# Moving the plain values of three batches behind the next scores, with other PSUM tiles for them and for the output, and a new order of VectorE's copies at the start

## The chip, the cores and the metric

The kernel runs on one core of one Trainium2 chip. A core has TensorE (PE: matrix products, with PEld its weight loads), VectorE (DVE), ScalarE (ACT), GpSimd (POOL) and SyncE (SP); each works through its own instructions in order, and semaphores hold one back until another has come far enough. Products are written to PSUM, eight banks of 2 KB in each of 128 partitions. The metric is device time in microseconds of one launch; the median of 3 runs of the kernel before is 308.29 us (308.21 to 308.9).

## The reference

Eight batches, 8 heads, 576 positions, head size 64: attention, then a two-layer network on all 4608 rows.

```python
rel = pos[:, None] - pos[None, :]
mask_plain = (rel >= 0) & (rel < 32)
mask_dil = (rel >= 0) & (rel < 32 * 4) & (rel % 4 == 0)
masks = np.stack([mask_plain if h < H // 2 else mask_dil for h in range(H)], axis=0)
scores = np.where(masks, scale * q @ k.T, -1e9)
attn = softmax(scores) @ v                  # each head
x = attn.transpose(0, 2, 1, 3).reshape(B * S, H * D)
h = x @ w_in                                # 512 -> 2048
out = (h * sigmoid(h)) @ w_out              # 2048 -> 512
```

Heads 0 to 3 see the last 32 positions ("plain"), heads 4 to 7 every fourth of the last 128 ("class": positions of one residue by four, where the mask is again a band of 32).

## The kernel before, in words

Each batch `b` has two halves of attention, `z` = 0 (plain) and `z` = 1 (class). A half goes through these steps:

- `scores(b, z)` (L500): 72 or 80 small products on TensorE with 64 rows and 32 columns of weights, into three tiles of the pool `ps`; VectorE then scales, masks and takes the maxima (L521 to L537).
- `exps` (L552) on ScalarE; `normal` (L574) on VectorE: reciprocal of the sums, then `pn`.
- `pn` is transposed to `pt`: for early batches on TensorE (`turn` L589, with the copy `turned` L598), later by a DMA on SP's queue (`turn_by_dma` L604).
- `values(b, z)` (L613): 64 small products, 64 by 64, of `pt` and `vw` into two tiles `x`, and by `last_values` (L679) 8 (plain) or 16 (class) more for the last 64 positions into two short tiles `xs`. `finish` (L709) and `last_finish` (L702) copy the four tiles into `xT`, the input of the network.

The network: `layer1(b, f)` (L721), `f` from 0 to 15, makes 8 products of 288 columns into a tile `h`, and ScalarE writes SiLU of it to `gT` (L734). `layer2(b, plan)` (L783) makes output tiles of 128 rows, `t`, counted by `x`: 16 products of 512 columns each into `o`; `store` (L777) copies `o` with VectorE (L780), and SP writes it out. Rows go by pairs of batches, so an even batch has four output tiles and an odd batch five.

The order is written by hand. `plan_of(b)` (L820) lists what else is issued in batch `b`: `at(s, fn, ...)` puts a call at step `s`; step `f` comes before `layer1(b, f)` (L1025), and steps from 16 on come before every fourth product of layer 2, four steps to an output tile (L795). At one step the calls run in the order of their `at`. TensorE runs layer 1 and 2 of batch `b` and, between their products, the attention of batches `b` + 1 and `b` + 2. In batches 3 to 5 that is: plain values of `b` + 1 at step 6 (L913), class scores of `b` + 1 at step 11 or 12, plain scores of `b` + 2 at step 17 (L920), class values of `b` + 1 at step 29 (L927), `normal` and `turn_by_dma` of the class half at steps 22 and 23 and of the plain half of `b` + 2 at 27 and 28 (L932).

PSUM is shared by two pools: `big` has two tiles of two banks (`h`, `o`, of which `o` uses the first bank), `ps` four tiles of one bank (scores, values). A tile that takes over a bank waits until the last reader of the tile there has finished.

Batch 0 starts with the attention of 288 rows in two parts (`masks0`, `scores0`, `values0` L642, `finish0` L670), while the weights are still on their way. `short_products` (L432) are small products of zeros that keep TensorE busy; 102 open the kernel (L942), and 14 stand before the sixth pair of `h` tiles (L1008). `shift_plain` (L195) is two copies on VectorE (L198, L200) that lay `v` beside itself for overlapping windows; in batch 0 the second set is at step -14 (L835), ahead of the copy `turned` at step -4 (L837).

Of the kernel before, what the change touches and what calls it, by code (L numbers as in the profile page):

```python
# [9 lines left out]
F32 = mybir.dt.float32  # L10
# [5 lines left out]
P = 128  # L16
# [4 lines left out]
QB = 32  # L21
# [8 lines left out]
def kernel(  # L30
# [10 lines left out]
    B, H, S, D = q.shape  # L41
# [7 lines left out]
    NM = NB // 2  # L49
# [4 lines left out]
    SA = NS // 2  # L54
# [555 lines left out]
            out=pt[:, 0 : w // 2], in_=a["pn", z, hi][:, 0:w].rearrange("p t c -> p (t c)")  # L610
        )

    def values(b, z):  # L613

        a = att(b)
        x = a["x", z] = [
            ps.tile([P, 2, SA], F32, tag="ps", name=f"x_{b}_{z}_{e}") for e in (0, 1)
        ]
        for i in range(8):
            for n in (0, 1):  # L620
                for e in (0, 1):
                    r = slice(e * KB, e * KB + KB)
                    for hi in (0, 1):
                        dst = x[e][hi * D : hi * D + D, n]
                        pt = a["pt", z, hi]
                        if z == 0:
                            j = 2 * i + e
                            w = plain_v(a, j, 2 * n + hi)
                            dst = dst[:, i * QB : (i + 1) * QB]
                            p = pt[r, 2 * n + j // 8, i % 4 * QB : i % 4 * QB + QB]  # L630
                        else:
                            m, c = i // 4, i % 4
                            w = class_v(a, 2 * m + e, 2 * n + hi, c)
                            dst = dst[:, m * P : (m + 1) * P].rearrange("d (i r) -> d r i", r=DIL)[:, c]
                            p = pt[r, 2 * n + m, c * QB : c * QB + QB]
                        nc.tensor.matmul(dst, w, p, start=True, stop=True)  # L636
        a["xs", z] = [
            ps.tile([P, 2, QB], F32, tag="ps", name=f"xs_{b}_{z}_{e}") for e in (0, 1)
        ]
        last_values(b, z, (0, 1))  # L640

    def values0(z, part):  # L642
# [134 lines left out]
    def store(o, row, name, m0=0, copy=nc.vector.tensor_copy, queue=nc.sync):  # L777
# [2 lines left out]
        copy(ob, o)  # L780
        queue.dma_start(out=out[row : row + P, m0 : m0 + m], in_=ob)

    def layer2(b, plan):  # L783

        tiles = range(0, 4) if b % 2 == 0 else range(4, 9)
        for x, t in enumerate(tiles):
            row = (b // 2) * 2 * S + t * P
            cut = 3 * DM // 4 if (b, t) == (B - 1, 8) else DM
            for m0, m1 in ((0, cut), (cut, DM)):
                if m0 == m1:  # L790
                    continue
                o = big.tile([P, 2, 512], F32, tag="big", name=f"o_{b}_{t}_{m0}")[:, 0, 0 : m1 - m0]
                for f in range(NFF):
                    if f % 4 == 0 and m0 == 0:
                        plan(NFF + 4 * x + f // 4)  # L795
                    nc.tensor.matmul(  # L796
                        o, gT[:, f, t * P : (t + 1) * P], w_out16[:, f, m0:m1],
                        start=(f == 0), stop=(f == NFF - 1),
                    )
                store(o, row, f"ob_{b}_{t}_{m0}", m0)  # L800
# [19 lines left out]
    def plan_of(b):  # L820
        ev = {}

        def at(s, fn, *args):
            ev.setdefault(s, []).append((fn, args))

        def all_exps(b, z):
            for hi in (0, 1):
                at(16, exps, b, z, hi)

        if b == 0:  # L830

            at(-14, normal, 0, 1, 1)
            at(-14, normal, 0, 0, 1)
            at(-14, shift_class, 0, dve, 1, 2)
            at(-14, shift_plain, 0, dve, 4, NM)  # L835
            at(-4, turn, 0, 0, 1)
            at(-4, turned, 0, 0, 1)  # L837
            at(-4, values0, 1, 1)
            at(-4, last_values, 0, 1, (1,))
            at(-4, finish0, 1, 1)  # L840
            at(-4, last_finish, 0, 1, 1)
            at(-2, values0, 0, 1)
            at(-2, last_values, 0, 0, (1,))
            at(-2, finish0, 0, 1, both)
            at(-2, last_finish, 0, 0, 1)
            at(-2, clear_short, 1, nc.vector)
            at(-2, load_v, 1)
            for c in (2, 3):
                at(-2, load_w_out, c)
            at(-2, load_qk, 2)  # L850
            transposes(at, 1, 1, 2)
            at(8, scores, 1, 1)
            for hi in (0, 1):
                at(8, shift, 1, 1, hi)
            for which in (1, 0):
                at(18, transpose, 1, 0, which, (dve, dve) if which else (act, act))
            at(20, normal, 1, 1, 0)
            at(20, scores, 1, 0)
            at(14, shift_v, 1, nc.sync.dma_start)
            at(18, load_rows, 3)  # L860
            at(18, load_v, 2)
            all_exps(1, 1)
            for hi in (0, 1):
                at(20, exps, 1, 0, hi)
            for n, z, hi in ((20, 1, 1), (26, 0, 0), (28, 0, 1)):
                at(n, normal, 1, z, hi)
            for n, z, copies in ((27, 1, (dve, dve)), (30, 0, both)):
                for hi in (0, 1):
                    at(n, turn, 1, z, hi)
                for hi in (0, 1):  # L870
                    at(n, turned, 1, z, hi, copies[hi])
                at(n + 1 + z, values, 1, z)
                at(n + 1 + z, finish, 1, z, both)
        elif b == 1:
            transposes(at, 2, 0, 3)
            transposes(at, 2, 1, 11)
            at(2, shift_v, 2, nc.sync.dma_start)
            for z in (0, 1):
                at(2, cross, 3, z)
                at(28, cross, 4, z)  # L880
            at(9, scores, 2, 0)
            for hi in (0, 1):
                at(12, shift, 2, 0, hi)
            at(17, load_v, 3)
            at(17, nc.gpsimd.tensor_copy, latch, qTs[1][:, 1, S - 1 : S])
            at(17, load_rows, 4)
            at(14, scores, 2, 1)
            all_exps(2, 0)
            all_exps(2, 1)
            for hi in (0, 1):  # L890
                at(19, normal, 2, 0, hi)
            at(21, scores, 3, 0)
            at(21, exps, 3, 0, 0)
            at(21, exps, 3, 0, 1)
            later(at, 2, 0, (None, None, 27, 28))
            later(at, 2, 1, (29, 31, 33, 34))
        else:
            if b + 2 < B:
                at(0, load_v, b + 2)
                if b + 3 < B:  # L900
                    at(0, load_rows, b + 3, (1, 0))
                if b + 3 < B:
                    at(12, cross, b + 3, 0)
                if b > 2:
                    at(12, cross, b + 2, 1)
            if b + 1 < B:
                at(1 if b == 2 else 0, shift_plain, b + 1, dve, 0, NM)
                at(12, shift_class, b + 1, dve, 0, 2)
                at(12, shift_over, b + 1, dve)
                if b == 2:  # L910
                    later(at, 3, 0, (0, 0, 4, 6))
                else:
                    at(6, values, b + 1, 0)  # L913
                    at(6, finish, b + 1, 0)
                x = {2: 13, 3: 12}.get(b, 11)
                at(x, scores, b + 1, 1)
                at(x, shift, b + 1, 1, 1)
                all_exps(b + 1, 1)
            if b + 2 < B:
                at(18 if b == 2 else 17, scores, b + 2, 0)  # L920
                for hi in (0, 1):
                    at(18, exps, b + 2, 0, hi)
            if b + 1 < B:
                for hi in (0, 1):
                    at(22 + hi, normal, b + 1, 1, hi)
                    at(22 + hi, turn_by_dma, b + 1, 1, hi)
                at(29, values, b + 1, 1)  # L927
                at(29, finish, b + 1, 1)
            if b + 2 < B:
                for hi in (0, 1):  # L930
                    at(27 + hi, normal, b + 2, 0, hi)
                    at(27 + hi, turn_by_dma, b + 2, 0, hi)  # L932

        def plan(s):
            for fn, args in ev.pop(s, ()):
                fn(*args)

        return plan


    busy = big.tile([P, 2, 512], F32, tag="big", name="busy")
    short_products(busy, 102)  # L942
    keep_busy(busy[:, 0], 8)
    masks0(1, 0)
    masks0(0, 0)
# [55 lines left out]
    for b in range(B):  # L1001
        plan = plan_of(b)
        if b == 0:
            for x in range(NFF):
                h = first[x] if x < 4 else None
                if x == 5:
                    h = big.tile([P, 2, 512], F32, tag="big", name=f"h_0_{2 * x}_0")
                    short_products(h, 14)  # L1008
                plan(2 * x - NFF)
                plan(2 * x + 1 - NFF)  # L1010
                tile = 2 * x % NFF, 2 * x // NFF
# [51 lines left out]
```

## Time and profile before

| What | Value |
|---|---|
| Median of 3 runs | 308.29 us |
| The profiled execution | 308.48 us, its span 306.7 us |
| PE busy | 298.1 us |
| ACT busy | 186.7 us |
| DVE busy | 180.8 us |
| Granted TensorE clock | 1.000 |
| Layer 1, products of L726 | 896, 113.5 us |
| Layer 2, products of L796 | 528, 114.3 us |
| Output copies of L780, VectorE | 35, mean 673 ns |

The span runs from the first to the last instruction of one execution that the hardware profiler recorded. Times of rows are microseconds from its start. A row of the timeline has start, length, engine, line, operation, out<-in, shape of the weights, shape of the output or operands, count, and in brackets how long the engine had been idle and what ended that. TensorE overlaps products, so lengths of its rows overlap, and a difference of two starts is what a run of products takes. An arrow like "<-PE o L796" names the instruction that released the wait.

### The profile page before, as it was taken

What the parts mean: (1) busy time and instruction counts of PE and PEld (TensorE: products, weight loads), DVE (VectorE), ACT (ScalarE), POOL (GpSimd) and SP (SyncE); (2) the same over time, 40 slices, a digit from 0 to 9 for tenths busy, and PEclk for the clock granted to TensorE, in tenths of its full rate; (3) what the DMA queues carried; (4) which work ended last, traced back from release to release, by engine and by line L of the source; (5) the groups of instructions that cost most, each with busy time, mean ns of one, the idle gap of its engine ahead of it and who ended that gap; (6) DMA issues with size and microseconds to landing.
All of it is one profiled execution on the core that took longest, in us unless ns stands there. A gap on an engine that the chain in (4) does not pass through costs nothing.

```text
span 306.7 us, 10605 instructions
## 1 busy us (share of the span) xinstructions
PE 298.1 (97%) x4591; PEld 189.2 (62%) x4591; DVE 180.8 (59%) x375; ACT 186.7 (61%) x554; POOL 92.3 (30%) x139
## 2 busy tenths in 40 slices
PE   8788999999999999999999999999999999999995
PEld 4466754677555875477644775467644775478543
DVE  7898579618797738953785348852885344620012
ACT  1757677776894558945792558945793558246200
POOL 8517455861462840096007610040000000000000
PEclk9999999999999999999999999999999999999999
DMA  8999999999999998499789995498026000400021
GB/s 105 169 204 203 189 205 203 154 211 179 148 151 192 163 202 108 128 149 175 104 152 169 194 118 105 130 139 118 4 75 145 34 4 7 139 36 2 3 100 71
DMA packets 104399, 39.00 MB, mean 127 GB/s; under 512 B 79504, under 2 KB 99600, under 8 KB 104352
## 3 DMA queue, kind: packets, MB, share of 16 engines
q0 software_dynamic: 63104, 18.88, 62.1%
q1 hardware_dynamic: 41248, 19.44, 29.3%
q8 instruction: 36, 0.59, 0.8%
q14 instruction: 11, 0.09, 0.1%
HBM read 37.75 MB, written 9.44 MB: 154 GB/s over the span
## 4 chain that ended last, share of the span: by engine, by line
PE 82%; DVE 9%; ACT 3%; DMA 3%; issue 1%; POOL 1%; POOLq 0%; SPq 0%; ACTq 0%
PE h L726 36%; PE o L796 29%; PE o L770 5%; PE h L746 4%; PE x L636 3%; DMA nat<-in_k_dram 2%; ACT pe L569 2%; DVE pn L585 2%; PE s L391 1%; DVE l L578 1%; PE s L379 1%; PE t L329 1%; DMA ptT<-pn 1%; DVE ms L521 1%; PE pt L594 1%
## 5 line engine op out<-in xcount | busy, mean ns | idle before, releaser
L734 ACT ACTIVATE gT<-h 128x576 f16<-128x576 f32 x112 | 72.9, 651 | 78.1 <-PE h L726 77.9
L796 PE MATMUL o<-w_out,gT 128*128 128x512 f16 (+2 forms) x528 | 114.3, 373 | 0.1
L726 PE MATMUL h<-xT,w_in 128*128 128x288 f16 x896 | 113.5, 286 | 0.0
L726 PEld LDWEIGHTS <-w_in 128*128 128x128 f16 x896 | 86.4, 98 | 23.3 <-DVE xT L713 0.3
L796 PEld LDWEIGHTS <-gT 128*128 128x128 f16 x528 | 50.0, 98 | 55.8 <-issue 0.3
L569 ACT ACTIVATE pe<-ms,nm 128x64 f32<-128x64 f32 x178 | 59.1, 333 | 2.8 <-DVE nm L537 2.7
L780 DVE COPY ob<-o 128x512 f32<-128x512 f32 (+2 forms) x35 | 23.5, 673 | 47.1 <-PE o L796 46.1
L521 DVE SCALAR_TENSOR_TENSOR ms<-s,mask 128x512 f32<-128x512 f32 x28 | 19.2, 685 | 35.5 <-PE s L391 24.7
L569 ACT ACTIVATION_READ_ACCUMULATOR pe<-ms,nm 128x1 f32 x178 | 33.2, 187 | 0.0
L713 DVE CAST xT<-x 128x512 f16<-128x512 f32 x26 | 16.8, 684 | 21.3 <-PE xs L700 21.3
L177 POOL DMA_DIRECT2D vw<-in_v_dram x16 | 10.1, 638 | 62.9 <-PE xs L700 62.0
L585 DVE TENSOR_TENSOR pn<-pe,r 128x640 f16<-128x640 f32 (+2 forms) x32 | 25.3, 791 | 1.1
L537 DVE TENSOR_REDUCE nm<-ms 128x10 f32<-128x640 f32 (+1 forms) x28 | 22.0, 787 | 1.0
L746 PE MATMUL h<-xT,w_in 128*128 128x256 f16 (+1 forms) x128 | 17.1, 286 | 0.8 <-DMA w_in<-in_moe_w_in_dram 0.6
L134 POOL DMA_DIRECT2D nat<-in_q_dram x20 | 14.8, 761 | 6.4 <-DMA nat<-in_k_dram 3.3
L134 POOL DMA_DIRECT2D nat<-in_k_dram x20 | 15.1, 760 | 5.0 <-DMA vw<-in_v_dram 3.8
L770 PE MATMUL o<-w_out,gT 128*128 128x512 f16 x64 | 15.2, 380 | 0.0
L746 PEld LDWEIGHTS <-w_in 128*128 128x128 f16 x128 | 11.8, 98 | 4.3 <-DMA w_in<-in_moe_w_in_dram 1.2
L758 ACT ACTIVATE gT<-h 128x512 f16<-128x512 f32 (+1 forms) x16 | 10.0, 653 | 6.0 <-PE h L746 5.8
L636 PEld LDWEIGHTS <-vw 64*64 64x64 f16 x896 | 8.5, 108 | 5.4 <-issue 5.3
L185 POOL DMA_DIRECT2D vw<-in_v_dram x16 | 9.3, 584 | 4.1 <-DVE r L582 1.7
L578 DVE TENSOR_REDUCE l<-pe 128x10 f32<-128x640 f32 (+2 forms) x12 | 9.6, 801 | 1.5 <-ACT pe L560 1.4
(102 smaller groups left out, 254.1 us busy)
## 6 DMA issues: line engine op xcount, KB each, us to landing
out_dram<-ob SPq DMA_DIRECT2D x35, 256.0 KB, 2.5
vw<-in_v_dram POOLq DMA_DIRECT2D x8, 288.0 KB, 7.8
vw<-in_v_dram POOLq DMA_DIRECT2D x16, 128.0 KB, 6.0
w_in<-in_moe_w_in_dram POOLq DMA_DIRECT2D x4, 512.0 KB, 12.9
w_out<-in_moe_w_out_dram POOLq DMA_DIRECT2D x4, 512.0 KB, 10.9
nat<-in_k_dram POOLq DMA_DIRECT2D x6, 256.0 KB, 7.5
nat<-in_q_dram POOLq DMA_DIRECT2D x6, 256.0 KB, 7.9
nat<-in_k_dram POOLq DMA_DIRECT2D x20, 72.0 KB, 7.2
```

The lines of the kernel that those rows point to most:

```text
L134: nc.gpsimd.dma_start(out=f[:, 2 * (1 - which) + h // 2, 0 : ZR - 1, h % 2], in_=src[b, h].rearrange("(m p) d -> p m d", p=RT),)
L521: nc.vector.scalar_tensor_tensor(out=ms[:, 0:8].rearrange("p (n t) c -> p n (t c)", n=2), in0=s[hi].rearrange("p n t c -> p n (t c)"), sca ...
L537: nc.vector.tensor_reduce(out=nm[:, 0:w], in_=ms[:, 0:w], axis=AX.X, op=ALU.max, negate=True)
L569: nc.scalar.activation(pe[:, t, :], slot(t), AF.Exp, scale=1.0 if b else scale, bias=nm[:, t : t + 1], accum_out=l[:, t : t + 1],)
L585: nc.vector.tensor_tensor(pn[:, 0:w], a["pe", z, hi][:, 0:w], r[:, 0:w, None].broadcast_to([P, w, KB]), ALU.mult)
L636: nc.tensor.matmul(dst, w, p, start=True, stop=True)
L726: nc.tensor.matmul(h[:, half, 0:HS], w_in16[:, c, f * P : f * P + P], xT[:, c, half * HS : half * HS + HS], start=(c == 0), stop=(c == MC ...
L734: nc.scalar.activation(gT[:, f, s0 : s0 + S].rearrange("p (a c) -> p a c", a=2), h[:, :, 0:HS], AF.Silu)
L746: nc.tensor.matmul(h[:, i, 0 : c1 - c0], w_in16[:, c, (f + i) * P : (f + i + 1) * P], xT[:, c, c0:c1], start=(c == 0), stop=(c == MC - 1),)
L770: nc.tensor.matmul(o, gT[:, f, t * P : (t + 1) * P], w_out16[:, f, :], start=(f == 0), stop=(f == NFF - 1),)
L780: copy(ob, o)
L796: nc.tensor.matmul(o, gT[:, f, t * P : (t + 1) * P], w_out16[:, f, m0:m1], start=(f == 0), stop=(f == NFF - 1),)
```

## The change

1. In batches 3, 4 and 5 (`merged`), `values(b + 1, 0)` goes from step 6 to step 17, right behind `scores(b + 2, 0)`, and its `finish` to step 24. Its two tiles `x` become the two banks of one `big` tile, and its first short tile `xs` lies in the second bank of the `big` tile that holds the first output tile.
2. In these batches output tiles 1 and 2 are taken from `ps`, and the fifth (`x` = 4, in batches 3 and 5) is the second bank of the tile whose first bank is the fourth output tile. So the output of such a batch takes two `big` tiles in place of four or five, and the values take one more.
3. There, `normal` and `turn_by_dma` of the second plain half of `b` + 2 go from step 28 to 30.
4. In batch 0 the second `shift_plain` goes from step -14 to -4, behind `turned`; `finish0(1, 1)` uses ScalarE for one of its two copies.
5. 100 short products open the kernel in place of 102, and the 14 before the sixth pair of `h` tiles are dropped.

```diff
+    pair = [None]
-    def values(b, z):
+    def values(b, z, beside=False):
         a = att(b)
-        x = a["x", z] = [
-            ps.tile([P, 2, SA], F32, tag="ps", name=f"x_{b}_{z}_{e}") for e in (0, 1)
-        ]
+        if beside:
+            both_x = big.tile([P, 2, 512], F32, tag="big", name=f"x_{b}_{z}")
+            x = [both_x[:, e].rearrange("p (n c) -> p n c", n=2) for e in (0, 1)]
+        else:
+            x = [ps.tile([P, 2, SA], F32, tag="ps", name=f"x_{b}_{z}_{e}") for e in (0, 1)]
+        a["x", z] = x
...
-        a["xs", z] = [
-            ps.tile([P, 2, QB], F32, tag="ps", name=f"xs_{b}_{z}_{e}") for e in (0, 1)
-        ]
+        if beside:
+            xs = [pair[0][:, 1, 0 : 2 * QB].rearrange("p (a c) -> p a c", a=2)]
+        else:
+            xs = [ps.tile([P, 2, QB], F32, tag="ps", name=f"xs_{b}_{z}_0")]
+        a["xs", z] = xs + [ps.tile([P, 2, QB], F32, tag="ps", name=f"xs_{b}_{z}_1")]
...
+    def merged(b):
+        return 2 < b < B - 2
...
-                o = big.tile([P, 2, 512], F32, tag="big", name=f"o_{b}_{t}_{m0}")[:, 0, 0 : m1 - m0]
+                if merged(b) and x in (1, 2):
+                    o = ps.tile([P, 512], F32, tag="ps", name=f"o_{b}_{t}")
+                elif merged(b) and x == 4:
+                    o = pair[0][:, 1]
+                else:
+                    pair[0] = big.tile([P, 2, 512], F32, tag="big", name=f"o_{b}_{t}_{m0}")
+                    o = pair[0][:, 0, 0 : m1 - m0]
...
-            at(-14, shift_plain, 0, dve, 4, NM)
             at(-4, turn, 0, 0, 1)
             at(-4, turned, 0, 0, 1)
+            at(-4, shift_plain, 0, dve, 4, NM)
...
-            at(-4, finish0, 1, 1)
+            at(-4, finish0, 1, 1, both)
...
-                else:
+                elif not merged(b):
                     at(6, values, b + 1, 0)
                     at(6, finish, b + 1, 0)
...
                 at(18 if b == 2 else 17, scores, b + 2, 0)
+                if merged(b):
+                    at(17, values, b + 1, 0, True)
+                    at(24, finish, b + 1, 0)
...
-                    at(27 + hi, normal, b + 2, 0, hi)
-                    at(27 + hi, turn_by_dma, b + 2, 0, hi)
+                    step = 27 + (3 if merged(b) else 1) * hi
+                    at(step, normal, b + 2, 0, hi)
+                    at(step, turn_by_dma, b + 2, 0, hi)
...
-    short_products(busy, 102)
+    short_products(busy, 100)
...
-                if x == 5:
-                    h = big.tile([P, 2, 512], F32, tag="big", name=f"h_0_{2 * x}_0")
-                    short_products(h, 14)
```

## The prediction

> **What bounds the kernel now.** I read the page first: the busy shares, the slices and the chain.
>
> ```profile
> span 306.7 us, 10605 instructions
> ...
> PE 298.1 (97%) x4591; PEld 189.2 (62%) x4591; DVE 180.8 (59%) x375; ACT 186.7 (61%) x554; POOL 92.3 (30%) x139
> ...
> PEclk9999999999999999999999999999999999999999
> ...
> PE 82%; DVE 9%; ACT 3%; DMA 3%; issue 1%; POOL 1%; POOLq 0%; SPq 0%; ACTq 0%
> ```
>
> TensorE is busy 97% of the span at full clock, and the slices below 9 lie in the first 20 us. So from about 30 us on, a change is worth what it takes from or adds to TensorE's own row of products and gaps; before that, which wait ends last. Next I read TensorE's timeline over batch 4, the middle one of the three that change.
>
> ```profile
> 174.83 0.69 PE L636 MATMUL x<-ptT,vw 64*64 64x32 f16 x64
> 175.36 0.22 PE L700 MATMUL xs<-ptT,vw 64*64 64x32 f16 x8
> 175.51 5.08 PE L726 MATMUL h<-xT,w_in 128*128 128x288 f16 x40
> ...
> 186.24 1.03 PE L796 MATMUL o<-w_out,gT 128*128 128x512 f16 x4
> 187.19 0.72 PE L379 MATMUL s<-plain 64*32 64x64 f16 x64
> 187.74 0.27 PE L379 MATMUL ss<-plain 64*32 64x64 f16 x8
> 187.94 10.53 PE L796 MATMUL o<-w_out,gT 128*128 128x512 f16 x48
> 198.40 0.71 PE L636 MATMUL x<-ptT,vw 64*64 64x32 f16 x64
> 198.93 0.32 PE L700 MATMUL xs<-ptT,vw 64*64 64x16 f16 x16
> 199.19 2.76 PE L796 MATMUL o<-w_out,gT 128*128 128x512 f16 x12
> 201.79 4.45 PE L726 MATMUL h<-xT,w_in 128*128 128x288 f16 x35
> ```
>
> The reader is to subtract starts, since a row's own length holds the drain. A product of layer 2 takes 0.216 us (199.19 to 201.79 for 12) and one of layer 1 0.1225 (15.68 us for the 128 that start at 270.40). The 4 products at 186.24 need 0.95 before the scores start, where 4 x 0.216 is 0.86: 0.09 us goes on entering the small tiles, at every such block. Leaving them costs 0.11 to 0.12 from the last small product's start.
>
> **Part 1: plain values behind the scores (batches 3, 4, 5 as b).** 72 small products leave step 6 of layer 1 and stand behind the 72 of the scores. Their own 0.68 us (174.83 to 175.51) is only moved. The entry at step 6 goes, 0.09. The step from the 64x32 tiles of the scores to the 64x64 tiles of the values takes the place of the scores' exit. No row shows that pair. The nearest is 64x128 to 64x64 at 6.6 us, where the last transpose is followed after 0.12 us; the other end is the 0.01 us between small products of one shape. I take 0.12, as the nearest in kind: nothing gained there, and 3 x 0.09 = **0.28 us gained** (at the other end 3 x 0.20 = 0.6). [...]
>
> What waits on them? With 0 at the first product of layer 2 (186.24), scores start at 0.96 and values at 1.65, end at 2.33, and output tiles then end at 4.92, 8.37, 11.82 and, with 0.79 of strided values inside, 16.15. On VectorE the four copies into xT (1.54 us by the rows from 199.65) now stand behind the second tile's copy: the first tile's copy starts at 5.1, the two class normalisations end at 9.15 (195.18 before, 0.2 later by the first tile's copy), second copy 9.75, xT copies 11.3, first plain normalisation 12.4, third copy 13.1. The strided values' second short tile takes the third tile's bank and is reached at 13.3: 0.2 us to spare. The strided xT copies end at 15.05, and the second plain normalisation, now at step 30, at 16.3, just as the fourth tile is ready (16.35). So VectorE is full but not late: cost nothing, 0.2 to 0.5 us a batch if the cover goes. Nothing else is queued behind it that TensorE wants earlier. That normalisation's transpose keeps its place on SP between the same two output stores. It lands 3.4 to 7.3 us after issue (four such rows), so by 24; its reader comes at 26.5 in batch 6 and much later in the others. The moved values and copies issue no DMA, and POOL's v loads wait for the strided values as before.
>
> **Part 2: output tiles in other banks.** Tiles 1 and 2 sit in one-bank tiles that the score copies have freed by 2.5 and 3.8; they start at 4.9 and 8.4. The fifth tile, in batches 3 and 5 only, goes into the second half of the large tile that holds the fourth. I read the order of the changed program with its waits: the fifth tile's first product waits for VectorE, for the copy of the fourth tile out of the other half. In before it waited for the copy of the tile two places earlier, long done. So TensorE now sits out a whole copy:
>
> ```profile
> 201.99 0.69 DVE L780 COPY ob<-o 128x512 f32<-128x512 f32 x1 [0.80 <-PE o L796]
> ```
>
> This copy, out of a last tile, starts 0.20 us after TensorE's next product did (201.79). 0.20 + 0.69 + 0.05 to wake TensorE (a copy that ends at 27.52 lets products start at 27.58, below) = 0.94 us idle. All of TensorE's queue is behind it, and the later batches follow TensorE, so nothing takes it up. Twice: **1.88 us lost**. It can't be much below 0.94 unless the wait is not there; above it by what VectorE is late (to 1.2).
>
> **Part 3: the start.** The timeline from 24 to 31 us tells it; VectorE's rows, then TensorE's:
>
> ```profile
> 25.81 0.42 DVE L205 COPY vw<-vw 32x1024 f16<-32x1024 f16 x1
> 26.15 0.48 DVE L198 COPY vw<-vw 32x1280 f16<-32x1280 f16 x1
> 26.64 0.48 DVE L200 COPY vw<-vw 32x1280 f16<-32x1280 f16 x1
> 27.05 0.47 DVE L602 COPY ptT<-pt 128x640 f16<-128x640 f16 x1
> ```
>
> ```profile
> 27.58 0.30 PE L700 MATMUL xs<-ptT,vw 64*64 64x16 f16 x8 [0.72 <-DVE ptT L602]
> 27.81 1.05 PE L746 MATMUL h<-xT,w_in 128*128 128x256 f16 x8
> ```
>
> The short values at 27.58 want a bank that the copy of pt gives back, and that copy stands behind two shifts of v, 0.90 us. In the change the copy goes first: pt is written at 26.27, the copy runs 26.31 to 26.78, and the values start at 26.83 instead of 27.58: 0.75. The shifts then end at 27.7 and one xT copy moves to ScalarE, which idles from 27.24 to 28.89, so VectorE ends this row at 28.3 instead of 28.45. With the rows' own distances (0.23 to the 8 products at 27.81, 0.98 to the next values, 0.43 and 0.88 to the first products of the second part) the next values start at 28.04 and the second part at 29.35 (30.10 before); VectorE's xT is ready at 29.2 (29.95 before). w_in's last quarter landed at 26.61 and the q for the transposes that move to 30.5 at 29.52. What TensorE waits for up to 60 us otherwise hangs on ScalarE or VectorE behind TensorE, and moves along; the nearest DMA margins there are over 1 us. So **0.75 us gained**, between 0 (a wait I have not seen takes it) and 0.8. The 14 short products dropped (0.16 us at 23.9) gain nothing: the values at 26.3 wait for ScalarE's copy (25.46 + 0.80, behind four SiLUs) and for the class shift. The two dropped at the head are 0.02 us ahead of a wait for data: nothing.
>
> **Sum.** 1.88 - 0.28 - 0.75 = +0.85 us. The profiled execution took 308.48 us (span 306.7, 1.78 around it); it would become 309.33. It lies 0.19 above the median of the runs, 308.29, so I predict 309.15.
>
> **Rivals.**
> - *The fifth tile is not held* (faster). The two halves are different banks, and a copy out of one need not hold products into the other. Then 1.88 goes: 308.29 - 1.03 = 307.25. For it: the banks differ. Against: the wait stands in the program, and TensorE runs in order. [...] Chance 0.06.
> - *No drain between the two small shapes* (no change measurable). 0.35 more is gained: 308.8. For it: both use 64 rows. Against: the 0.12 at 6.6 us, also between shapes of 64 rows. With smaller gains of this size elsewhere: 0.18.
> - *The start gives nothing back*: a DMA or ScalarE is late instead, 309.9. Against: the margins above. Chance 0.10.
> - *VectorE is late in layer 2*: the third tile's copy after 13.3, or the fourth's after 16.35; it decides when VectorE slips by 0.2 us, and costs some 0.2 us in each of three batches: 309.75. Chance 0.10.
>
> My forecast has 0.56. The likely cases lie from 308.5 (no drain, and somewhat less idle) to 310.0 (late VectorE with a start that gives little): that range leaves out the first rival and as much again. A measurement of this kernel tells 0.2%, 0.62 us, from no change. Faster 0.07, same 0.20, slower 0.73.
>
> **What would show it.** In the changed profile: a gap of some 0.94 us on TensorE ended by VectorE's output copy, twice, before 16 products of a fifth tile in batches 3 and 5, and none in batch 4; the block of 72 + 72 small products with about 0.12 us between the shapes; layer 1 with 48 + 40 products unbroken where the values stood; the short values near 26.8. No such gap would make the forecast wrong, and so would a gap at the strided values in three batches or a new wait between 28 and 60 us.

## The result, and the profile after

The median of 6 runs is 313.11 us (311.03 to 314.03); the kernel before took 308.88 us beside it (308.21 to 311.28). The ratio is 1.0117, with an interval of 1.0080 to 1.0154. The sign was as forecast (309.15), the size was not: the range ended at 310.0. The profiled execution is the longest of the six, 314.03 us, because its granted clock was below full for a while (0.50 from 16.14 to 22.97 us, 0.989 over the span). It was below full (under 0.998) in 34 of 89 later runs of the kernel before too, and in three of the six here; the three at full clock took 311.03 to 312.55 us, still some 2 to 3 us above the forecast. A ratio leaves out runs more than 1.5% above the fastest of their kernel, and it is not the quotient of the two medians, which count all runs.

From the page of the kernel after, the lines that answer to those of before, and the row of the queue that brings instructions:

```profile
span 312.0 us, 10574 instructions
...
PE 300.3 (96%) x4575; PEld 191.4 (61%) x4575; DVE 179.7 (58%) x374; ACT 187.2 (60%) x555; POOL 93.1 (30%) x139
...
PEclk9959999999999999999999999999999999999999
...
q8 instruction: 35, 0.57, 0.8%
...
PE 83%; DVE 6%; ACT 4%; DMA 3%; issue 2%; POOL 0%; ACTq 0%; SPq 0%; POOLq 0%
```

Three things stand out. PE is busy 2.2 us longer, though it has 16 products fewer. One slice has half the clock. And "issue", time in which an engine waits for nothing that the profile shows, has gone from 1% of the chain to 2%.

I then took the start of each stage in both traces (layer 1 and layer 2 of each batch, to the start of the last product: 303.33 us before, 308.61 after) and subtracted:

| Stretch | After minus before, us |
|---|---|
| up to layer 1 of b = 1 (starts at 58.93 and 59.49) | +0.56 |
| layer 1 of b = 1 (19.03, 21.70) | +2.67 |
| layer 1 of b = 3, 4, 5 (17.32, 17.38, 17.32; each 16.53 to 16.66) | -2.30 |
| layer 2 of b = 3, 4, 5 (19.01, 15.55, 18.93; 20.63, 16.46, 20.61) | +4.21 |
| all else | +0.14 |

**The fifth tile.** TensorE's row and VectorE's in the timeline of after, b = 3:

```profile
166.06 2.76 PE L812 MATMUL o<-w_out,gT 128*128 128x512 f16 x12
...
168.86 0.69 DVE L787 COPY ob<-o 128x512 f32<-128x512 f32 x1
169.60 1.67 PE L812 MATMUL o<-w_out,gT 128*128 128x512 f16 x7 [0.78 <-DVE ob L787]
```

Twelve products should end their turn at 166.06 + 12 x 0.216 = 168.65; the next one starts at 169.60, 0.05 after VectorE's copy. That is 0.95 us, and 0.94 in b = 5: 1.89 of the 4.21.

**The merged block.** TensorE's rows of after in layer 2 of b = 4, to be held against the rows at 186.24 to 199.19 before:

```profile
190.67 0.68 PE L379 MATMUL s<-plain 64*32 64x64 f16 x64
191.16 0.40 PE L379 MATMUL ss<-plain 64*32 64x64 f16 x8
191.49 0.81 PE L641 MATMUL x<-ptT,vw 64*64 64x32 f16 x64
...
192.29 10.53 PE L812 MATMUL o<-w_out,gT 128*128 128x512 f16 x48
202.75 0.71 PE L641 MATMUL x<-ptT,vw 64*64 64x32 f16 x64
203.34 0.30 PE L707 MATMUL xs<-ptT,vw 64*64 64x16 f16 x16
```

The scores and values stand in one block, here of 1.62 us (1.37 in b = 5, 223.67 to 225.04). Behind them the class values reach their short tiles 0.59 us after they start (202.75 to 203.34), where it was 0.53 before (198.40 to 198.93).

**The new loss** lies where the change touches nothing: in the 72 transposes for batch 2, in layer 1 of b = 1. First before, then after:

```profile
61.99 0.83 PE L329 MATMUL t<-ident,nat 64*64 64x64 f16 x72
```

```profile
62.55 0.54 PE L329 MATMUL t<-ident,nat 64*64 64x64 f16 x44
65.41 0.41 PE L329 MATMUL t<-ident,nat 64*64 64x64 f16 x28 [2.31 <-issue]
```

TensorE stops for 2.5 us, from the start of the 44th transpose to that of the 45th (the row counts 2.31 from the modelled end), and no semaphore releases it. I numbered TensorE's instructions in the order of the program (a weight load and its product are two) and call the number the position. This stop is at position 2498, and a smaller one, 0.3 us, at 2754, exactly 256 later; both are 194 above a multiple of 256. The queue called "instruction" moved 35 packets of 16 KB here and 36 before, as many as the positions that are 194 above a multiple of 256 in the 9150 and 9182 of the two kernels: one for every 256 (their times are read from the DMA records of the trace). The packet after position 2242 was passed (at 58.05 us) is moved at 62.98 to 63.87 us, and TensorE goes on 1.5 us after its end. So my first theory was: TensorE ran out of instructions. The 16 short products that the change drops had moved every later position by 32.

**The clock** is lost at the start. In this execution the 8 products of layer 1 at 18.60 take 1.81 us, where they took 0.97 before (18.11 to 19.08); the granted clock from 18.60 to 20.40 is 0.50:

```profile
18.60 1.89 PE L753 MATMUL h<-xT,w_in 128*128 128x256 f16 x8
20.41 0.55 PE L379 MATMUL s<-plain 64*32 64x64 f16 x40
```

The half clock lasts from 16.14 to 22.97 us. It hides what VectorE's new order gained there, so that part needs a run of its own.

### The profile page after: what moved, and what is told of

Same layout as the page of the kernel before. It is cut to its first block, busy times and chain, and to the rows that moved or that the text cites. A ratio compares the mean times of both kernels' runs of the same rounds, so it can differ in the third digit from the quotient of the medians.

```text
span 312.0 us, 10574 instructions
## 1 busy us (share of the span) xinstructions
PE 300.3 (96%) x4575; PEld 191.4 (61%) x4575; DVE 179.7 (58%) x374; ACT 187.2 (60%) x555; POOL 93.1 (30%) x139
## 4 chain that ended last, share of the span: by engine, by line
PE 83%; DVE 6%; ACT 4%; DMA 3%; issue 2%; POOL 0%; ACTq 0%; SPq 0%; POOLq 0%
PE h L733 36%; PE o L812 29%; PE o L777 5%; PE h L753 4%; PE x L641 3%; DMA nat<-in_q_dram 2%; ACT pe L569 2%; PE s L391 2%; PE s L379 1%; DVE pn L585 1%; PE t L329 1%; DVE ob L787 1%; DMA ptT<-pn 1%; PE pt L594 1%; DVE l L578 1%
## 5 line engine op out<-in xcount | busy, mean ns | idle before, releaser
L733 PEld LDWEIGHTS <-w_in 128*128 128x128 f16 x896 | 86.6, 98 | 23.4 <-DVE xT L720 0.3
L753 PE MATMUL h<-xT,w_in 128*128 128x256 f16 (+1 forms) x128 | 18.6, 306 | 0.0
L753 PEld LDWEIGHTS <-w_in 128*128 128x128 f16 x128 | 12.9, 104 | 3.9
L641 PE MATMUL x<-ptT,vw 64*64 64x32 f16 x896 | 10.3, 187 | 0.2 <-DMA ptT<-pn 0.2
```

Source lines behind the costliest of these rows:

```text
L733: nc.tensor.matmul(h[:, half, 0:HS], w_in16[:, c, f * P : f * P + P], xT[:, c, half * HS : half * HS + HS], start=(c == 0), stop=(c == MC ...
L753: nc.tensor.matmul(h[:, i, 0 : c1 - c0], w_in16[:, c, (f + i) * P : (f + i + 1) * P], xT[:, c, c0:c1], start=(c == 0), stop=(c == MC - 1),)
```

## The experiments

For a stop, "edge" is a position that is 194 above a multiple of 256. Ratios are to the kernel before on the same chip, with their intervals; stage lengths are from the profiled execution of each kernel.

**1. The fifth tile in a tile of its own** (the changed kernel, nothing else different):

```diff
-                if merged(b) and x in (1, 2):
+                if merged(b) and x in (1, 2, 4):
...
-                elif merged(b) and x == 4:
-                    o = pair[0][:, 1]
```

> The changed kernel with one edit: the fifth output tile of batches 3 and 5 in a one-bank tile of its own, so that its first product no longer waits for the copy of the fourth. The instructions of every engine stay in number and order. My theory (two idle stretches of 0.94 us, as the profile after shows them): both go, 1.9 us less than the changed kernel, so 309.2 to 309.5 in executions at full clock. Rival (the gaps were hidden slack, later waits take them up): less than 0.5 us gained. The stop of 2.4 us inside the transposes of batch 2 (at 63 us) and a lower clock at 16 to 22 us have nothing to do with it and may both stay.

309.82 us (307.99 to 312.14, 12 runs), ratio 1.0023 (0.9992 to 1.0054). Both gaps of 0.94 us are gone, and layer 2 of b = 5 takes 19.67 us instead of 20.61. The stop at 2498 stays, 1.4 us. The false wait was real, and it was not all.

**2. The changed kernel with 16 short products more at the opening**, so that positions are again those of before:

```diff
-    short_products(busy, 100)
+    short_products(busy, 116)
```

> The changed kernel with 116 short products of zeros at the head in place of 100, so that every later instruction of TensorE stands 32 places further on in its stream, as in the kernel before; the 14 stay away from their old place. Theory (the stop of 2.4 us at 63 us is TensorE waiting for its next 16 KB of instructions, whose edge fell 88 instructions into the block of 72 transposes and is 32 later in before): the edge moves back, the stop goes or shrinks under 0.5 us, and the kernel takes 308.9 to 309.4 at full clock. Rival (it is the earlier traffic that the new order of VectorE brings, wherever the edge is): the stop stays, 311. If dropping products at the head is also what lowers the clock at 16 us, the clock is 1.0 here in all executions; if that is chance or comes from elsewhere, it is lower in some.

312.21 us (310.89 to 314.0, 9 runs), ratio 1.0097 (1.0068 to 1.0126). The stop in layer 1 of b = 1 is gone (19.09 us). But two others have come, "issue" again: 1.1 us at position 5570 and 2.0 us at 6594, each just behind a merged block. Both are edges. So the time did not fall to the 308.9 to 309.4 us expected, and the merged block had become a suspect.

**3. Only the 16 short products dropped** from the kernel before:

```diff
-    short_products(busy, 102)
+    short_products(busy, 100)
...
-                if x == 5:
-                    h = big.tile([P, 2, 512], F32, tag="big", name=f"h_0_{2 * x}_0")
-                    short_products(h, 14)
```

> The kernel before with part 5 of the change alone: 100 opening products, and the 14 gone. My prediction gave this part nothing, 308.3. Theory of the instruction edge: the block of transposes at 62 us now holds the edge 32 instructions deeper, and a stop of 1 to 2.5 us appears there, 309.3 to 310.8. Rival (traffic): no stop, 308.3. The clock: lower at 16 to 22 us in some executions if the dropped products cause that.

310.32 us (307.88 to 314.14, 12 runs), ratio 1.0004 (0.9969 to 1.0040): the runs alone decide nothing. The trace does: a stop of 1.3 us at 2498, behind the 44th transpose as in the changed kernel, with 0.3 us at 2754, and layer 1 of b = 1 at 20.46 us. Nothing else of the change was in this kernel.

**4. Only VectorE's order at the start**, in the kernel before:

```diff
-            at(-14, shift_plain, 0, dve, 4, NM)
...
+            at(-4, shift_plain, 0, dve, 4, NM)
...
-            at(-4, finish0, 1, 1)
+            at(-4, finish0, 1, 1, both)
```

> The kernel before with part 4 alone: the second pair of shifts behind the copy of pt, and one xT copy on ScalarE. TensorE's stream is unchanged. Prediction: 0.75 us gained, 307.5. Rival (traffic: the earlier start meets the instruction fetch at 58 to 63 us): a stop at 62 us takes it back, 308.5 to 310. The clock at 16 us lies ahead of this edit and should be as in before.

308.16 us (307.57 to 310.56, 12 runs), ratio 0.9954 (0.9924 to 0.9983). Its timeline on TensorE, to be held against the rows at 27.58 and 27.81 before:

```profile
26.56 0.35 PE L700 MATMUL xs<-ptT,vw 64*64 64x16 f16 x16
26.87 1.05 PE L746 MATMUL h<-xT,w_in 128*128 128x256 f16 x8
27.84 0.49 PE L662 MATMUL x<-ptT,vw 64*64 64x32 f16 x31
28.52 0.20 PE L662 MATMUL x<-ptT,vw 64*64 64x32 f16 x1 [0.18 <-issue]
```

The wait before the short values is gone, and the next values start at 27.84 instead of 28.79, 0.95 earlier. Then an edge (1218) holds their last product back by some 0.4 us, and the second part starts at 29.60 instead of 30.10: 0.5 is left.

**5. The merged block with both other faults mended** (fifth tile of its own, the 102 and 14 short products as before): the edits of run 1, and those of run 3 undone.

> The changed kernel with two things mended: the fifth tile of layer 2 in a tile of its own, and the 16 short products back (102 at the opening, 14 in layer 1 of batch 0). What is left of the change is the merged block and VectorE's order. Theory (instructions arrive in packets of 256 of TensorE's, and a packet that comes late stops TensorE where the next 256 begin, which is at stream positions of 194 above a multiple of 256): no stop in layer 1 of b=1 (19.0 to 19.1 us), no gap of 0.94 us, but stops behind the merged block again at the same stream positions as with the 16 put back, 5570 and 6594, of 1 to 2 us each, so layer 2 of b=3 near 20.7 and of b=4 near 18.2 us, and a median near 310.5 us. Rival (the stops came from the fifth tile's wait or from the opening): no stop over 0.3 us anywhere, layer 2 of b=3 19.7 and of b=4 16.2 us, and a median of 307.9 us, the 308.0 of VectorE's order alone less 0.05 for each merge.

310.59 us (308.91 to 313.81, 12 runs), ratio 1.0044 (1.0007 to 1.0081). As expected: layer 1 of b = 1 takes 19.04 us, and the stops are at 5570 (2.1 us) and 6594 (1.0 us). The first of them in the timeline:

```profile
150.93 0.82 PE L810 MATMUL o<-w_out,gT 128*128 128x512 f16 x3
153.71 11.34 PE L810 MATMUL o<-w_out,gT 128*128 128x512 f16 x45 [1.96 <-issue]
```

Three products behind the block, at position 5570, TensorE stops; the packet is moved at 151.36 to 152.46. And 45 products at 0.216 us would take 9.7 us; they take 11.3, since several run at 0.427, half the clock (0.994 granted over the span). Layer 2 of b = 3 comes to 23.26 us. In b = 5 the edges fall otherwise, nothing stops, and layer 2 takes 19.67: what a merged batch costs without stops.

**6. The same with the values 12 full products behind the scores**, so that there is no block of 144 small products:

```diff
-                    at(17, values, b + 1, 0, True)
+                    at(20, values, b + 1, 0, True)
```

> The kernel of the run beside it (fifth tile of its own, 16 short products back) with the plain values 12 full products (2.6 us) behind the plain scores, so that the 144 small products don't stand in one block; they still go to a large tile, and the stream positions are the same. Theory (the dense block uses up a packet of 256 instructions before the next has come): the stops at positions 5570 and 6594 go or shrink below 0.3 us; each of the three batches pays a second entry and exit of small tiles, 0.2 us, so layer 2 of b=3 near 19.9, of b=4 near 16.4 us, and a median near 308.3 us. Rival (large tile or the order of the copies is what stops TensorE): stops of 1 to 2 us stay in b=3 and b=4, median 310 to 311 us.

310.26 us (309.35 to 312.22, 12 runs), ratio 1.0040 (1.0010 to 1.0071). No stop of a microsecond behind the block, but my own edit brought another wait: at step 20 the first output tile is complete, and the short values, in the other half of its large tile, stand 0.4 to 0.6 us behind its copy, in all three batches (layer 2 of b = 5: 20.40 us). It is the false wait of the fifth tile in another place.

**7. Run 3 with the loads called later** (batch 3's rows and batch 2's values at step 31 instead of 18):

```diff
-            at(18, load_rows, 3)
-            at(18, load_v, 2)
+            at(31, load_rows, 3)
+            at(31, load_v, 2)
```

> The kernel before without its 16 short products (this stopped TensorE for 1.29 us at stream position 2498), and with the loads of batch 3's rows and batch 2's values issued 13 steps (some 11 us) later, so that GpSimd's transfers are no longer queued where position 2242 is passed, at 57.4 us. Theory (the packet with the next instructions was served 4 us after position 2242 because these transfers were ahead of it): it is served within 2 us, no stop at 2498, layer 1 of b=1 19.0 to 19.1 us, and full clock runs near 308.8 us. Rival (the place alone, or the opening, makes the stop, not the transfers): a stop of 1 to 2 us stays in layer 1 of b=1 (20.3 us or more).

312.26 us (310.04 to 314.42, 6 runs), ratio 1.0102 (1.0043 to 1.0161). The edit missed: GpSimd is held by data and not by TensorE's steps, so it still issued the loads from 49 us on. It was run 3 once more, and the stop at 2498 came again, 2.9 us, with the packet served at 64.18 to 65.12.

**8. Run 6 with 8 products between**, where no copy is pending: `at(19, values, b + 1, 0, True)`.

> The split kernel once more, with the plain values 8 full products (1.7 us) behind the plain scores instead of 12, still inside the first output tile: no copy of that tile is pending, so the large tile's second half need not wait (12 products behind, the first 32-wide product of the class part stood 0.4 to 0.6 us behind the copy of the first half). Theory (packets of 256 instructions; a dense block uses one up before the next has come): no stop over 0.3 us at stream positions 5570 and 6594, no wait of 0.4 us inside the block, layer 2 of b=3 and 5 19.9 us and of b=4 16.4 us, median 308.0 + 3 x 0.15 = 308.5 us. Rival (something else about the values in the large tile costs time): layer 2 of b=3 and 5 stays at 20.4 us, median 310 us.

309.55 us (308.04 to 311.50, 12 runs), ratio 1.0000 (0.9971 to 1.0029). The false wait is gone (layer 2 of b = 5: 19.78 us), but the stops are back, at 5570 (1.5 us) and 6594 (1.0 us). My expectation of none was wrong: 1.7 us more between the two edges was not enough. Edge 5314 was passed at 150.54 and TensorE went on past 5570 only at 155.06.

**9. Run 3 with the loads held back by data**, by an instruction on GpSimd that reads the last plain values of batch 1:

```diff
+            at(31, lambda: nc.gpsimd.tensor_copy(latch, state[1]["xT"][:, 0, 0:1]))
```

with the two calls behind it.

> The kernel before without its 16 short products, and the loads of batch 3's rows and batch 2's values held on GpSimd by an instruction that reads what the last plain values of batch 1 leave (at 58 us). Moving the calls alone had not moved the issues, which ran on from 49 us. So GpSimd's transfers are now issued from some 58 us on instead of from 49 us. Theory (the packet with the next 256 instructions stood behind these transfers): it is served by 60 us, no stop at stream position 2498, layer 1 of b=1 19.0 to 19.1 us (unless the rows come too late for the scores of batch 3, some 82 us). Rival (the place of the edge alone makes the stop, however loaded the queues are): a stop of 1.3 us or more at 2498, layer 1 of b=1 20.3 us or more.

316.20 us (315.58 to 317.40, 6 runs), ratio 1.0215 (1.0175 to 1.0255). The loads are now issued from 60.8 us on. The packet is served at 59.98 to 60.90, and the transposes run through; the price is that the rows come too late for the scores of batch 3:

```profile
63.32 0.83 PE L329 MATMUL t<-ident,nat 64*64 64x64 f16 x72
...
88.05 0.68 PE L379 MATMUL s<-plain 64*32 64x64 f16 x64 [4.27 <-DMA plain<-nat]
```

Same 16 products missing, same edges, no stop at 2498: with GpSimd's transfers away, the packet is moved 1.1 us after 2242 was passed; in runs 1, 3 and 7 and in the changed kernel, with them on their way, it took 3.8 to 5.3 us. So, by this one trace, the transfers are part of the cause.

**10. Dense blocks alone**, in layer 1 of b = 6, where DMA is busy 2% of the time: 64, 128 and 256 short products added to the kernel of run 4, whose edits are not shown again.

```diff
+        short_products(h, {(6, 2): 64, (6, 8): 128, (6, 14): 256}.get((b, f), 0))
```

> The cost measured by itself, in a stage whose DMA share is 0.02 (layer 1 of b=6, 238 to 255 us): the kernel before with VectorE's order, and 64, 128 and 256 added short products (two TensorE instructions each) ahead of the products of hidden blocks 2, 8 and 14. By the opening's 102 of them in 0.9 us, they take 0.6, 1.1 and 2.3 us with entry and exit. Theory (256 instructions come in one packet, of about 1 us, with about 1.5 us behind it before TensorE goes on, also in quiet queues): behind 64 no stop, behind or in 128 a stop of 0.3 to 1.5 us, in 256 one or two stops that sum to 2 us or more, each at a stream position of 194 above a multiple of 256. Rival (only loaded queues make a packet late): no stop over 0.2 us in any of the three.

315.96 us (2 runs), ratio 1.0200 (1.0137 to 1.0264), with work added. 64 took 0.58 us and 128 took 1.11, without a stop. But no edge falls into the 64, and only one into the 128 (8386, at 247.30, 3.0 us after the one before), so they say little about the length of a block. The 256:

```profile
254.90 1.57 PE L437 MATMUL h<-zero 64*32 64x16 f16 x175
258.82 0.80 PE L437 MATMUL h<-zero 64*32 64x16 f16 x81 [2.35 <-issue]
259.55 4.02 PE L727 MATMUL h<-xT,w_in 128*128 128x288 f16 x16
```

A stop of 2.5 us at position 9154, an edge, in quiet queues. The 16 products behind it take 3.8 us instead of 2.0. From a window view of the same kernel (the columns after TensorE, its weight loads, VectorE, ScalarE and GpSimd are the granted clock, the DMA share and GB/s):

```profile
259.00:262.00 3.00, 3.00 (x91) 2.10 (x69) 0.00 (x0) 0.31 (x1) 0.00 (x0) 0.50 0.02 5
```

The clock is at half: the 2.5 us of the stop are followed by 1.8 us more in these products. That loaded queues are needed, the rival, is refuted; that 128 might stop did not come true.

**11. Run 5 with the edges moved**: 56 more short products at the opening, 112 positions.

```diff
-    short_products(busy, 102)
+    short_products(busy, 158)
```

> The merged kernel with its own fifth tile and the 16 short products (it stopped for 2.1 us behind the block of b=3 and 1.0 us behind that of b=4), and 56 more short products of zeros at the opening, where TensorE waits for data for 3 us anyway. All later work is moved by 112 stream positions, so the edges (194 above a multiple of 256) fall 181 to 212 instructions into the merged blocks of b=3, 4 and 5 instead of 37 to 68; the edge before lies 22 to 37 full products ahead of the block, and the next some 80 products behind it. Theory (only the spacing in time of two edges counts, 3.6 us or more is enough in quiet queues): no stop in b=3, 4, 5, layer 2 of them 19.7, 16.3 and 19.7 us, layer 1 of b=1 19.0 to 19.1 us, and at full clock 0.1 to 0.2 us below VectorE's order alone, in the run beside it. Rival (a dense block of 288 small instructions stops TensorE wherever the edge lies): stops of 1 us or more stay in b=3 and b=4.

The first block again:

```profile
153.67 0.18 PE L707 MATMUL xs<-ptT,vw 64*64 64x32 f16 x2
153.79 10.53 PE L810 MATMUL o<-w_out,gT 128*128 128x512 f16 x48
```

No stop; layer 2 of b = 3, 4, 5 takes 19.67, 16.33 and 19.71 us, and layer 1 of b = 1 19.04, to the tenth what was expected. But the time is 314.37 us (310.68 to 318.84, 6 runs), ratio 1.0156 (1.0109 to 1.0202): the edges now fall badly at the start, with new stops at positions 706 (0.7 us), 962 (1.8 us) and 1474 (1.0 us), and 5 of the 6 runs lost clock (0.978 to 0.995 granted over the span). I had looked at the blocks from 57 us on only.

**12. Run 4 again**, beside run 11.

> VectorE's order alone once more, beside the merged kernel with moved edges, so that the two are compared on one chip: by its first run 0.7 us below before (0.9954 of it), no stop at any edge, and 0.1 to 0.2 us above the merged kernel if that one does not stop.

308.64 us (307.49 to 309.53, 12 runs), ratio 0.9989 (0.9966 to 1.0012). The second part starts at 29.65 us in the trace, as in the first run, but the gain in time is not repeated. One edge has a stop that was not expected, 0.5 us at 6338 (180.30 to 180.76). Between the two runs, VectorE's order brings something from nothing to 0.8 us. No version tried beats the kernel before in every comparison.

## Why the prediction was wrong

**The step that failed** is the sentence on the dropped short products: "The 14 short products dropped (0.16 us at 23.9) gain nothing", and nothing for the two at the head. As time on TensorE they are nothing. But without them all later positions move by 32, and another instruction stands at each edge, the place of the stops in the table below. The kernels without them have the stop at 2498 (2.5, 1.4, 1.3 and 2.9 us in the changed kernel and runs 1, 3, 7), unless GpSimd's transfers are out of the way (run 9); no kernel with positions as before has it (before, runs 2, 4, 5, 6, 8, 10, 12). I looked for what waited on the products' time and never asked what else counts them. The list of signs watched for a new wait from 28 to 60 us; this one lies at 62.9.

These are the stops of 1 us or more behind 57 us in all the traces that no semaphore ends, with the time at which the edge before was passed (in run 8 at 6594 the profile names VectorE's maxima, but these had ended at 192.16, 0.26 us before TensorE went on):

| Kernel, edge | Edge before passed | Packet moved | TensorE goes on |
|---|---|---|---|
| after, 2498 | 58.05 | 62.98 to 63.87 | 65.41 |
| run 1, 2498 | 58.90 | 62.65 to 63.55 | 65.11 |
| run 3, 2498 | 57.51 | 61.42 to 62.35 | 63.63 |
| run 7, 2498 | 58.90 | 64.18 to 65.12 | 66.63 |
| run 2, 5570 | 149.83 | 150.26 to 151.41 | 152.89 |
| run 2, 6594 | 188.06 | 189.74 to 190.70 | 192.06 |
| run 5, 5570 | 149.62 | 151.36 to 152.46 | 153.71 |
| run 5, 6594 | 189.42 | 189.95 to 190.84 | 192.29 |
| run 8, 5570 | 150.54 | 151.84 to 153.31 | 155.06 |
| run 8, 6594 | 188.41 | 190.22 to 191.18 | 192.42 |
| run 10, 9154 | 255.24 | 256.18 to 257.52 | 258.82 |

In these rows it takes 2.9 to 4.5 us from one edge to the first instruction past the next in the later stages (3.6 in quiet queues) and 6.1 to 7.7 us at 58 us, among GpSimd's transfers. 256 positions of full products take 28 us (128 x 0.216), longer than any of these; a block of 144 small ones is 288 positions in some 1.4 us (1.37 in the changed kernel's b = 5).

One link is not shown. Dropping the 16 products did not bring the edges 2242 and 2498 closer in time: TensorE takes 4.8 us between them in before (57.37 to 62.21) and in run 3 (57.51 to 62.36). What differs is the packet. In the eight traces with positions as before it starts to move at most 1.6 us after 2242 was passed (58.56 in before), although GpSimd's transfers are on their way there too; without the 16 it starts 3.8 to 5.3 us after in four traces, and 1.1 us after in run 9, one trace, where the transfers are issued later. Passing later is not it: run 8, with the old positions, passes 2242 at 57.60, later than run 3. Why a shift of the edge by 32 positions makes the packet late among the transfers is open.

The other steps, in their order:

- **Part 1, 0.28 us gained: mis-sized.** The change of shape costs 0.120 us (191.366 to 191.486, from the last score product to the first of the values in b = 4 of the changed kernel), as taken, and not the 0.01 of the other end. But a merged batch without stops gains 0.79 in layer 1 and gives 0.74 back in layer 2 (19.67 against 18.93), 0.05 and not 0.09. That is less by about what the class values behind lose between their two shapes, 0.06 us. Three batches bring 0.15. With that the block has a price that the working did not have: whether it stops TensorE hangs on where the edges fall (2.5 us of stops in run 8, some 3.1 in runs 2 and 5, none in run 11). In the changed kernel itself it does not stop; b = 4 loses 0.2 us to small gaps inside its block (16.46 against 16.26 in run 1), whose cause I have not followed.
- **"VectorE is full but not late": right.** VectorE ends no gap of TensorE in the three batches but the fifth tile's (two, 1.6 us from the modelled ends).
- **Part 2, 1.88 us lost: right**, 1.89, with its mechanism and its place, and gone with a tile of its own (run 1).
- **Part 3, 0.75 us gained: right in mechanism, too large.** The wait is gone, the values behind it 0.95 earlier; 0.5 is left at the second part, since an edge falls there (run 4). In time it is not settled. In the changed kernel's profile half a clock of 6.8 us hides it.
- **The rivals.** None held. All four stayed within the waits that semaphores explain, and so did the range. The 0.2% that a measurement was taken to tell was too fine: with 12 runs the intervals reach 0.23 to 0.37% to each side.

The sum with what was measured, by traces: 1.89 - 0.15 - 0.50 + 2.7 for the stops at 2498 and 2754 = +3.9 us on the profiled execution's 308.48, 312.4 us (an estimate worked out from one trace of each kernel), close to the runs of the changed kernel at full clock (311.03 to 312.55). The profiled run of 314.03 adds the clock, some 1.1 us by the start of layer 1 of b = 1 (59.49, where run 4 has 58.41). In the other runs the length of the stop isn't known; run 3, whose own ratio is 1.0004, says that it is not 1.6 us in every execution.

**What stays open:** whether the start loses clock more often because of the change. Three of 6 runs of after did, 7 of 12 in run 1, 5 of 6 in run 11 and 5 of 6 in run 7, but only 3 of 12 in run 3, which gives TensorE the same instructions as run 7, 1 of 9 in run 2, and 34 of 89 runs of before.

## What to carry to other kernels

When a change adds, drops or gathers many small products, count instructions beside time: find the positions where the instruction packets are cut (194 above a multiple of 256 here), and look at the time between two of them and at when the packet is moved. The runs give no fixed bound: 3.0 us between two edges passed without a stop once (run 10, the block of 128), while TensorE needed 2.9 to 4.5 us at the stops in the later stages and up to 7.7 among GpSimd's transfers. A wait that the profile calls "issue" inside a run of small products, at positions that are a packet apart, was such a stop here; the stops moved when earlier products were added or dropped (runs 3 and 11), so a fix in one place must be checked at all others. And in this kernel a half of a tile was guarded like the whole: what shared a tile waited for the other half's reader (0.94 us a time, and 0.4 to 0.6 in run 6).

## What the runs showed of the hardware

- TensorE's instructions came in packets of 16 KB, one for 256 positions (35 packets in the changed kernel, 36 before), and TensorE went on 1.2 to 1.8 us after a late packet's end (the table). The stops were up to 2.9 us long (run 7).
- Some stops were followed by half the clock: 2.1 us of stop in run 5 (products at 0.427 us behind it), 2.5 us in run 10 (0.50 in the window). Those stretches of half clock lasted 3.41 and 6.83 us (0.994 and 0.989 granted over the spans of 310.6 and 315.1 us). The 2.5 us in the changed kernel at 63 us were not: the granted clock was 1.00 from 62 to 80 us.
